# Attention and SwiGLU in one kernel: v's first loads issued by GpSimd, the planner's model of transfers in flight, and new ranks

## The chip, the cores and the metric

The kernel runs on one core of a Trainium2 chip. The metric is the device time of one execution in microseconds. Engines are named as in the profile: PE is TensorE (PEld its weight loads), DVE is VectorE, ACT is ScalarE, POOL is GpSimd, SP is SyncE, which only issues DMA transfers here. A name with a q behind it (SPq) is that engine's instruction queue.

## The reference

Attention over 8 batches of 8 heads, sequence 576, head size 64, with a mask that is causal in blocks of 64; its output, put side by side by heads, goes through a gated feed-forward layer on 4608 tokens of width 512, inner width 1536.

```python
scores = scale * np.matmul(q, k.transpose(0, 1, 3, 2))
mask = (pos[:, None] // 64) >= (pos[None, :] // 64)
scores = np.where(mask, scores, -1000000000.0)
attn = np.exp(scores - np.max(scores, axis=-1, keepdims=True))
attn = attn / (np.sum(attn, axis=-1, keepdims=True) + 1e-09)
o = np.matmul(attn, v)                         # [8, 8, 576, 64]
x = o.transpose(0, 2, 1, 3).reshape(4608, 512)
g = x @ w_gate                                 # [512, 1536]
out = (g * (1.0 / (1.0 + np.exp(-g))) * (x @ w_val)) @ w_out
```

q, k and v are 32-bit floats; the three weights are 64-bit and arrive as pairs of 32-bit words.

## The kernel before

**Work.** Attention goes by pairs of heads. The first two batches are cut into two stretches of the sequence, columns 0 to 256 and 256 to 576, so that the feed-forward layer can begin on the first 256 tokens; the other batches go whole. For the first stretch of batch 0 (four head pairs), each pair does this: q and k are loaded (line 401; q on SP's queue, k on ACT's), turned by TensorE (line 425) and copied out of PSUM by ACT (line 433); the scores are products on TensorE (line 451), masked by ACT (line 493); the maximum over the keys, which lie along the partitions, is taken by copies and maxima (lines 496, 716, 719) and then by POOL with one all-reduce over partitions for each of the two heads (line 723); DVE subtracts (line 747), ACT takes the exponential (line 751); TensorE multiplies with v and with ones, for the sums (line 829); DVE inverts and divides (lines 858 to 865); the result is split into a rounded part and a rest (lines 345 and 348).

**v.** `load_v` (lines 768 and 773) brings v of one head pair, two transfers of 64 KB for the stretch 0 to 256. There are two tiles for v at that time, each with room for two such pairs.

**Weights.** Each of 12 slices of the three weights is 512 KB, loaded at line 953 into one of five raw tiles, one after another; ACT and DVE put the two words of each number together (lines 968 to 982) and split it into a rounded part and a rest (lines 987 and 990). The split w_out is stored to memory (lines 1006 and 1009) and read again later (line 1176).

**Feed-forward.** 18 tiles of 256 tokens. Each takes three products for a weight block: rounded by rounded, rounded by rest, rest by rounded (lines 1109 to 1111 for the gate and the value, 1201 to 1203 for the output), with ACT and DVE between them (lines 1143 to 1159).

**Order.** Every step is a task with an engine, a cost in microseconds, a rank and the buffers that it needs. `in_order` plays the whole program through once, while the kernel is built: each engine in turn takes, of the tasks that are ready and have buffers, the one with the lowest rank, and the order so found is the order of each engine's instructions. The chip then runs each engine strictly in that order. Ranks are numbers written at the top: FIRST for the head pairs of the cut stretches, V_OF added to them for v, AHEAD and PIECES for the weights, SIDE for the first tiles' feed-forward, SHIFT, LATER, LEAD and EAGER for attention further back. PATIENCE bounds how long a run of feed-forward products may keep others waiting, `spare` how early a buffer may be counted on. Most buffers are handed out in the order in which they were first named (IN_TURN). A transfer costs its issuing engine 0.5 us an issue in the plan and lands after the share of the DMA engines that its size takes:

```python
if t.moves:
    queue = max(queue, end + 0.65) + t.moves
    done = queue + t.late
```

**Fillers.** Where the plan leaves TensorE a gap of over 0.3 us, `keep_busy` puts small matmuls of ones into it (line 1418), by the gap's length, that nothing reads.

Of the kernel before, what the change touches and what calls it, by code (L numbers as in the profile page):

```python
# [18 lines left out]
def kernel(  # L19
# [17 lines left out]
    nc = tc.nc  # L37
# [3 lines left out]
    P = 128  # L41
# [4 lines left out]
    SP = NKC * P  # L46
# [3 lines left out]
    XT = 256  # L50


    LEAD, EAGER = 6.5924, 0.1229

    SUMS = 2

# [3 lines left out]

    FINE = 4

    AHEAD = {(0, 0): -7.0107, (0, 1): 36.1085, (0, 2): -18.8912, (1, 0): 31.7427, (1, 1): -31.9799, (1, 2): 0.9815}
    SHIFT = {2: (7.4686, 5.1562, 10.9114, -4.5382), 3: (1.9556, -4.9491, 4.9621, -5.9019)}
    LATER = 10.5257
    V_OF = {0: (-22.086, 29.9358, 35.7938, -10.0705), 256: (-24.4193, 26.1695, 18.0768, -3.5685)}

    PIECES = [
        (-21.3689, -13.7546, 20.5567),
        (11.7941, 27.8219, -4.5726),  # L70
        (49.6885, 13.4156, 26.3321),
        (11.7183, 15.2197, -1.7579),
        (-18.0985, -44.9945, -47.4415),
        (31.6729, 24.8955, 16.7936),
        (60.2941, 42.2325, 2.1654),
        (-33.4359, -22.1211, 23.695),
        (-12.0038, 4.2143, -2.4693),
        (-8.6318, -21.6194, -14.638),
        (-12.3513, 22.147, -26.7278),
        (-43.9322, -25.5975, 15.0576),  # L80
    ]

    SIDE = (-30.9587, 40.07)

    PATIENCE = 63.9495
    FILL = 0.6

    FIRST = {
        0: [(0, 256, (-51.44, -5.5901, -6.4061, 10.6381)), (256, 576, (-51.1247, -24.9988, -31.7586, 0.8861))],
        1: [(0, 256, (6.1693, 18.1885, 17.2184, -3.8483)), (256, 576, (-0.9978, 12.9756, 15.3541, 29.1059))],  # L90
    }
    TILES = [XT] * (NT // XT)

# [220 lines left out]
    for i in range(7):  # L314
        n = 2**i
# [9 lines left out]
    if wide:  # L325
        for place in range(len(slots["ob"])):
            t = tiles_of("ob", place, "signs")[0].bitcast(F32).rearrange("p m t -> p (m t)")
# [28 lines left out]
    def attention(R, b, h, a, e, early, bufs, lane):  # L356
# [404 lines left out]

        ps = Buf("at", also=banks)

        def load_v():
            nf = e // P
            for j, hd in enumerate(heads):
                cols = slice(j * D, (j + 1) * D)
                nc.sync.dma_start(
                    out=vt[0][:, 2 * lane : 2 * lane + nf, cols],
                    in_=v[b, hd, 0 : nf * P].rearrange("(c p) d -> p c d", p=P),  # L770
                )
            if e > nf * P:
                nc.sync.dma_start(
                    out=vt[0][0 : e - nf * P, nf, :].rearrange("p (h d) -> p h d", h=2),
                    in_=v[b, h : h + 2, nf * P : e].rearrange("h p d -> p h d"),
                )

        vl = dma(R + ((V_OF[a][h // 2] if b == 0 else LATER) if early else 0.0), 512.0 * e, load_v, [], [vt], 3 if e % P else 2, packet=256)
        segs = [s for s in ((0, 2 * P), (2 * P, S)) if a <= s[0] and s[1] <= e]
        ends = []  # L780
        direct = b == 0
# [516 lines left out]
    def in_order():  # L1298


        import heapq

        engines = ("PE", "POOL", "DVE", "ACT", "SP")
        idle = {e: 0.0 for e in engines}
        could = {e: [] for e in engines}
        room = {tag: [(0.0, i) for i in range(len(s))] for tag, s in slots.items()}
        turn = dict.fromkeys(slots, 0)
        events = [0.6]
        for t in tasks:
            if not t.waits:  # L1310
                could[t.engine].append(t)
        order = []
        now = queue = 0.0
        mode, last, stage, two = "", None, "", False

        WARM = 7.0
        CHANGE = {
            "": {"columns": 0.1, "rows": 0.2},
            "up": {"down": 0.02, "split": 0.01, "columns": 0.13, "rows": 0.2},
            "down": {"up": 0.072, "split": 0.01, "columns": 0.13, "rows": 0.2},  # L1320
            "split": {"up": 0.072, "down": 0.05, "columns": 0.13, "rows": 0.2},
            "columns": {"up": 0.195, "down": 0.2, "split": 0.2, "rows": 0.19, "turn": 0.15},
            "rows": {"up": 0.195, "down": 0.2, "split": 0.2, "columns": 0.13, "rows": 0.04, "turn": 0.15},
            "turn": {"up": 0.04, "down": 0.04, "split": 0.04, "columns": 0.13, "rows": 0.2},
        }

        spare = {"PE": 0.5218, "DVE": 0.7384, "ACT": 0.6046, "POOL": 0.0, "SP": 0.0}

        def place(t, by):

            need, turns = [], dict(turn)
            for u in t.bufs:
                if u.place is not None:
                    continue
                if u.tag in IN_TURN and u.n != turns[u.tag]:
                    return False
                turns[u.tag] += 1
                for tag in (u.tag, *u.also):
                    free = [f for f in room[tag] if f[0] <= by and (tag, f) not in need]
                    if free:  # L1340
                        need.append((tag, min(free)))
                        break
                else:
                    return False
            new = [u for u in t.bufs if u.place is None]
            for u, (tag, f) in zip(new, need):
                turn[u.tag] += 1
                room[tag].remove(f)
                u.tag, u.place = tag, f[1]
            return True  # L1350

        while events:
            now = heapq.heappop(events)
            while events and events[0] <= now:
                heapq.heappop(events)
            for e in engines:
                if idle[e] > now:
                    continue
                cand = sorted(
                    (t for t in could[e] if t.ready <= now),  # L1360
                    key=lambda t: (not t.mode or t.mode != mode, t.rank, t.n)
                    if mode and e == "PE"
                    else (t.rank, t.n),
                )
                if e == "DVE" and idle["POOL"] > now:
                    cand = [t for t in cand if not t.port]
                if e == "POOL" and idle["DVE"] > now and two:
                    continue

                if e == "PE":  # L1370
                    spot = min(((f, tag, i) for tag in ("at", "gv", "po") for f, i in room[tag]), default=(now, "", 0))
                follow = [(now, t) for t in cand if t.prev is not None and t.prev is last]
                if any(t.ready < now - PATIENCE for t in cand):
                    follow = []
                for by, t in (*follow, *((by, t) for by in (now - spare[e], now) for t in cand)):
                    if t.ready <= by and place(t, by):
                        break
                else:
                    continue
                could[e].remove(t)  # L1380
                order.append(t)
                end = now + t.cost
                if e == "PE":
                    key = t.mode or t.stage
                    end, mode, last, stage = end + CHANGE[stage].get(key, 0.0), t.mode, t, key
                    t.gap, t.at, t.spot = now - max(idle[e], spot[0], 0.6), now, spot[1:]
                    if now < WARM:
                        end += end - now
                if e == "DVE":
                    two = t.port  # L1390
                idle[e] = end
                heapq.heappush(events, end)
                done = end + (0.2 if e == "PE" else 0.13)
                if t.moves:
                    queue = max(queue, end + 0.65) + t.moves
                    done = queue + t.late
                heapq.heappush(events, done)
                for u in t.bufs:
                    u.left -= 1
                    u.free_at = max(u.free_at, done)  # L1400
                    if not u.left:
                        room[u.tag].append((u.free_at, u.place))
                        heapq.heappush(events, u.free_at)
                for x in t.next:
                    x.waits -= 1
                    x.ready = max(x.ready, end if x.engine == e == "PE" else done)
                    if not x.waits:
                        could[x.engine].append(x)
        left = [t for e in engines for t in could[e]]
        assert len(order) == len(tasks), (len(order), len(tasks), [(t.engine, t.rank, t.fn.__qualname__) for t in left][:10])  # L1410
        return order
# [42 lines left out]
```

## Time and profile before

| what | value |
|---|---|
| median of 3 runs | 1167.11 us (1166.97 to 1167.42) |
| the profiled execution | 1170.11 us, its span 1168.3 us |
| TensorE busy | 1153.5 us, 99% of the span |
| VectorE, ScalarE, GpSimd busy | 743.6, 619.6, 321.1 us |
| moved by DMA | 197.44 MB, mean 169 GB/s |
| granted TensorE clock over the run | 0.997 |

Busy time of an engine is the time in which the profiler shows an instruction on it; matmuls overlap, so a busy TensorE need not be at its peak. The fillers count as busy. A row of the timeline gives start, duration, engine, line, operation, tiles, and in brackets how long the engine stood before it and what ended that. A DMA row on a queue shows the issue, not the landing. A row by stretches gives the stretch, its length, the busy time of each engine with the number of instructions, the granted TensorE clock as a share of full speed, the share of the 16 DMA engines and GB/s.

### The profile page before, as it was taken

How to read it: one execution, taken by the hardware profiler on the slowest of the kernel's cores; microseconds unless marked ns; L12 is line 12 of the kernel's file. 1: busy time of each engine (PE TensorE's matmuls, PEld its weight loads, DVE VectorE, ACT ScalarE, POOL GpSimd, SP SyncE). 2: the span in 40 equal slices, each digit the busy share in tenths (PEclk: the TensorE clock that was granted, in tenths of full speed). 3: DMA queues.
4: the chain of work that ended last, by engine and by line, in shares of the span. 5: the costliest groups of instructions: out<-in, count | busy, mean ns of one | idle time of the engine just before them, and what ended most of it. 6: DMA issues, size and time to landing. Idle time of an engine off the chain costs nothing.

```text
span 1168.3 us, 22310 instructions
## 1 busy us (share of the span) xinstructions
PE 1153.5 (99%) x8744; PEld 1038.0 (89%) x8744; DVE 743.6 (64%) x1230; ACT 619.6 (53%) x1114; POOL 321.1 (27%) x141
## 2 busy tenths in 40 slices
PE   7999999999999999999999999999999999999998
PEld 6778788889899989898998989898998989999997
DVE  4998898877697857576774747576575643323222
ACT  5889776745675655473745555473655422212111
POOL 3213100153525263334133423333133420000000
PEclk8999999999999999999999999999999999999999
DMA  7857756766557466653756565663664445444352
GB/s 185 228 153 213 192 189 226 213 197 170 159 150 210 116 183 181 195 151 114 189 166 197 140 182 144 199 159 123 175 196 149 144 142 170 145 162 138 142 172 100
DMA packets 266986, 197.44 MB, mean 169 GB/s; under 512 B 195264, under 2 KB 231376, under 8 KB 266880
## 3 DMA queue, kind: packets, MB, share of 16 engines
q1 hardware_dynamic: 264304, 195.29, 57.3%
q8 instruction: 69, 1.13, 0.4%
q10 hardware_dynamic: 2576, 0.72, 0.3%
q14 instruction: 37, 0.30, 0.1%
HBM read 171.57 MB, written 24.38 MB: 168 GB/s over the span
## 4 chain that ended last, share of the span: by engine, by line
PE 91%; ACT 4%; DMA 2%; DVE 2%; issue 1%; POOL 0%; SPq 0%; POOLq 0%; ACTq 0%
PE gv L1109 17%; PE gv L1111 16%; PE gv L1110 16%; PE at L829 8%; PE po L1201 8%; PE po L1203 7%; PE po L1202 7%; PE at L578 6%; PE at L451 1%; ACT sc L469 1%; PE at L1201 1%; DMA wo<-in_moe_w_gate_dram 1%; PE at L1202 1%; PE at L1203 1%; PE at L662 1%
## 5 line engine op out<-in xcount | busy, mean ns | idle before, releaser
L723 POOL PARTITION_ALL_REDUCE mx<-mx x80 | 140.6, 1805 | 395.3 <-DVE mx L719 184.6
L1109 PE MATMUL gv<-xhl,v_all 128*128 128x256 f32 x864 | 241.2, 279 | 0.1
L880 POOL PARTITION_ALL_REDUCE mx<-mx x48 | 178.3, 3768 | 228.2 <-DVE mx L719 214.6
L1111 PE MATMUL gv<-xhl,v_all 128*128 128x256 f32 x864 | 239.1, 277 | 0.0
L1110 PE MATMUL gv<-xhl,v_all 128*128 128x256 f32 x864 | 239.0, 277 | 0.0
L1146 DVE SCALAR_TENSOR_TENSOR t<-t,gv 128x512 f32<-128x512 f32 x108 | 73.9, 684 | 164.4 <-ACT t L1143 163.8
L1109 PEld LDWEIGHTS gv<-xhl,v_all 128*128 128x128 f32 x864 | 162.1, 188 | 3.5 <-issue 1.6
L1110 PEld LDWEIGHTS gv<-xhl,v_all 128*128 128x128 f32 x864 | 162.2, 188 | 0.5
L1111 PEld LDWEIGHTS gv<-xhl,v_all 128*128 128x128 f32 x864 | 162.2, 188 | 0.0
L1156 ACT CAST hhl<-t 128x512 fp32r<-128x512 f32 x108 | 67.1, 622 | 165.0 <-PE po L1202 93.5
L1201 PE MATMUL po<-wo,hhl 128*128 128x512 f32 x372 | 147.5, 397 | 0.0
L1203 PE MATMUL po<-wo,hhl 128*128 128x512 f32 x372 | 145.2, 390 | 0.3 <-DVE hhl L1159 0.3
L1202 PE MATMUL po<-wo,hhl 128*128 128x512 f32 x372 | 145.5, 391 | 0.0
L1159 DVE TENSOR_TENSOR hhl<-t,hhl 128x512 fp32r<-128x512 f32 x108 | 82.2, 763 | 90.3 <-ACT hhl L1156 90.0
L747 DVE TENSOR_TENSOR sc<-sc,mx 128x640 f32<-128x640 f32 (+6 forms) x168 | 122.8, 772 | 16.2 <-POOL mx L723 16.0
L1143 ACT ACTIVATE t<-gv 128x512 f32<-128x512 f32 x108 | 64.6, 598 | 119.3 <-PE gv L1111 114.3
L1151 DVE SCALAR_TENSOR_TENSOR t<-t,gv 128x512 f32<-128x512 f32 x108 | 73.9, 684 | 81.6 <-PE gv L1111 80.8
L1109 PE MATMUL gv<-xhl,g_even 128*128 128x256 f32 x432 | 123.8, 286 | 0.0
L751 ACT ACTIVATE sc<-sc 128x1024 f32<-128x1024 f32 (+3 forms) x104 | 105.7, 1032 | 31.8 <-DVE sc L747 31.2
L1111 PE MATMUL gv<-xhl,g_even 128*128 128x256 f32 x432 | 122.1, 283 | 0.0
L1110 PE MATMUL gv<-xhl,g_even 128*128 128x256 f32 x432 | 122.1, 283 | 0.0
L1109 PE MATMUL gv<-xhl,g_odd 128*128 128x256 f32 x432 | 120.5, 279 | 0.0
(173 smaller groups left out, 2465.9 us busy)
## 6 DMA issues: line engine op xcount, KB each, us to landing
wo<-wo_d SPq DMA_DIRECT2D x200, 512.0 KB
out_dram<-ob SPq DMA_DIRECT2D x35, 256.0 KB
v<-in_v_dram SPq DMA_DIRECT2D x64, 128.0 KB
xt<-x_d SPq DMA_DIRECT2D x64, 128.0 KB
rt<-r_d SPq DMA_DIRECT2D x128, 64.0 KB
qk<-in_q_dram SPq DMA_DIRECT2D x112, 72.0 KB
qk<-in_k_dram SPq DMA_DIRECT2D x104, 72.0 KB
x_d<-xu SPq DMA_DIRECT2D x24, 288.0 KB
```

What stands on the lines that cost most here:

```text
L723: nc.gpsimd.partition_all_reduce(m, m, channels=P, reduce_op=bass_isa.ReduceOp.max)
L747: nc.vector.tensor_tensor(piece(c), scores_of(c), m, ALU.subtract)
L751: nc.scalar.activation(x, x, AF.Exp)
L829: nc.tensor.matmul(ps[0][own(x), 1 - i if sums else i, q0 - s0 : s1 - s0], lhsT=ones if sums else vt[0][:, 2 * lane + c, own(x)], rhs=sc[0 ...
L880: nc.gpsimd.partition_all_reduce(m, m, channels=P, reduce_op=bass_isa.ReduceOp.add)
L1109: nc.tensor.matmul(o, lhsT=hi[:, d], rhs=xhi[:, 0:w], start=first, stop=False)
L1110: nc.tensor.matmul(o, lhsT=hi[:, d], rhs=xlo[:, 0:w], start=False, stop=False)
L1111: nc.tensor.matmul(o, lhsT=lo[:, d], rhs=xhi[:, 0:w], start=False, stop=last)
L1159: nc.vector.tensor_tensor(hh[1][:, 0:n], t[0][:, 0:n], hh[0][:, 0:n].bitcast(F32), ALU.subtract)
L1201: nc.tensor.matmul(po, lhsT=hi, rhs=whi, start=i + y == 0, stop=False)
L1202: nc.tensor.matmul(po, lhsT=hi, rhs=wlo, start=False, stop=False)
L1203: nc.tensor.matmul(po, lhsT=lo, rhs=whi, start=False, stop=i + y == NFC - 1)
```

## The change

Three things are done, all of them to what is issued where and in which order; no arithmetic is added or removed.

1. `load_v` takes its queue as an argument: for batch 0, stretch 0 to 256, GpSimd issues the eight transfers; all others stay on SP. The task is booked on POOL.
2. `in_order` keeps a list of eight times, `in_flight`. A transfer is played issue by issue: issue number n by SP or ACT starts no sooner than the landing of issue number n - 8. An issue by POOL costs twice the time and takes no part in the turns.
3. All ranks, LEAD, EAGER, LATER, PATIENCE, SIDE and `spare` have new values.

```diff
-    LEAD, EAGER = 6.5924, 0.1229
+    LEAD, EAGER = 5.2695, 1.0637
-    AHEAD = {(0, 0): -7.0107, (0, 1): 36.1085, (0, 2): -18.8912, (1, 0): 31.7427, (1, 1): -31.9799, (1, 2): 0.9815}
+    AHEAD = {(0, 0): -7.1143, (0, 1): 32.7291, (0, 2): -26.4529, (1, 0): 32.2582, (1, 1): -17.6111, (1, 2): -3.3862}
-    LATER = 10.5257
-    V_OF = {0: (-22.086, 29.9358, 35.7938, -10.0705), 256: (-24.4193, 26.1695, 18.0768, -3.5685)}
+    LATER = 3.3066
+    V_OF = {0: (-30.1506, 37.9633, 41.0176, -1.7015), 256: (-24.6985, 17.6488, 41.1206, -0.1297)}
...
-    PATIENCE = 63.9495
+    PATIENCE = 39.3039
...
-        0: [(0, 256, (-51.44, -5.5901, -6.4061, 10.6381)), (256, 576, (-51.1247, -24.9988, -31.7586, 0.8861))],
+        0: [(0, 256, (-55.7558, -1.8175, -4.7037, 13.4226)), (256, 576, (-49.0629, -29.9958, -41.3412, 1.2806))],
...
-        def load_v():
+        def load_v(queue=nc.gpsimd if b == a == 0 else nc.sync):
...
-                nc.sync.dma_start(
+                queue.dma_start(
...
-        vl = dma(R + (...), 512.0 * e, load_v, [], [vt], 3 if e % P else 2, packet=256)
+        vl = dma(R + (...), 512.0 * e, load_v, [], [vt], 3 if e % P else 2, "POOL" if b == a == 0 else "SP", 256)
...
+        in_flight, issued = [0.0] * 8, 0
...
-        spare = {"PE": 0.5218, "DVE": 0.7384, "ACT": 0.6046, "POOL": 0.0, "SP": 0.0}
+        spare = {"PE": 0.4096, "DVE": 0.7262, "ACT": 0.5782, "POOL": 0.0, "SP": 0.0}
...
                 end = now + t.cost
+                if t.moves:
+                    end, n = now, max(1, round(t.cost / 0.5))
+                    for _ in range(n):
+                        if e == "POOL":
+                            end += 2 * t.cost / n
+                            queue = max(queue, end + 0.65) + t.moves / n
+                            landed = queue + t.late
+                            continue
+                        end = max(end, in_flight[issued % 8]) + t.cost / n
+                        queue = max(queue, end + 0.65) + t.moves / n
+                        landed = in_flight[issued % 8] = queue + t.late
+                        issued += 1
...
                 if t.moves:
-                    queue = max(queue, end + 0.65) + t.moves
-                    done = queue + t.late
+                    done = landed
```

SHIFT, PIECES, SIDE and the rows of FIRST for batch 1 change in the same manner.

More of the change, by code (lines that the diff above doesn't have):

```diff
@@ L61 @@
     FINE = 4
-    AHEAD = {(0, 0): -7.0107, (0, 1): 36.1085, (0, 2): -18.8912, (1, 0): 31.7427, (1, 1): -31.9799, (1, 2): 0.9815}
-    SHIFT = {2: (7.4686, 5.1562, 10.9114, -4.5382), 3: (1.9556, -4.9491, 4.9621, -5.9019)}
-    LATER = 10.5257
-    V_OF = {0: (-22.086, 29.9358, 35.7938, -10.0705), 256: (-24.4193, 26.1695, 18.0768, -3.5685)}
+    AHEAD = {(0, 0): -7.1143, (0, 1): 32.7291, (0, 2): -26.4529, (1, 0): 32.2582, (1, 1): -17.6111, (1, 2): -3.3862}
+    SHIFT = {2: (1.75, -1.1716, 38.593, -6.5525), 3: (-4.8263, -5.9467, 11.997, -5.7384)}
+    LATER = 3.3066
+    V_OF = {0: (-30.1506, 37.9633, 41.0176, -1.7015), 256: (-24.6985, 17.6488, 41.1206, -0.1297)}
     PIECES = [
[L69 to L80, printed above, removed]
-    ]
-    SIDE = (-30.9587, 40.07)
-    PATIENCE = 63.9495
+        (-42.2477, -7.4078, 31.321),
+        (19.6584, 26.4752, -1.1002),
+        (45.1975, 13.7804, 42.9148),
+        (31.3974, 30.3821, -10.0232),
+        (-19.9421, -49.9897, -51.8768),
+        (32.5027, 18.8486, 12.5049),
+        (80.4454, 43.4201, 8.0835),
+        (-36.0942, -27.2001, 36.8872),
+        (-7.1654, 5.1657, -7.2183),
+        (-16.086, -25.0859, -4.9908),
+        (-16.2853, 35.6967, -8.3972),
+        (-54.782, -30.9951, 38.7919),
+    ]
+    SIDE = (-20.2791, 49.5735)
+    PATIENCE = 39.3039
     FILL = 0.6
     FIRST = {
-        0: [(0, 256, (-51.44, -5.5901, -6.4061, 10.6381)), (256, 576, (-51.1247, -24.9988, -31.7586, 0.8861))],
-        1: [(0, 256, (6.1693, 18.1885, 17.2184, -3.8483)), (256, 576, (-0.9978, 12.9756, 15.3541, 29.1059))],
+        0: [(0, 256, (-55.7558, -1.8175, -4.7037, 13.4226)), (256, 576, (-49.0629, -29.9958, -41.3412, 1.2806))],
+        1: [(0, 256, (3.4577, 25.759, 16.3827, -11.2353)), (256, 576, (-5.3054, 10.4811, 13.1627, 43.7195))],
     }
@@ L772, in load_v @@
             if e > nf * P:
-                nc.sync.dma_start(
+                queue.dma_start(
                     out=vt[0][0 : e - nf * P, nf, :].rearrange("p (h d) -> p h d", h=2),
@@ L776, in load_v @@
                 )
-        vl = dma(R + ((V_OF[a][h // 2] if b == 0 else LATER) if early else 0.0), 512.0 * e, load_v, [], [vt], 3 if e % P else 2, packet=256)
+        vl = dma(R + ((V_OF[a][h // 2] if b == 0 else LATER) if early else 0.0), 512.0 * e, load_v, [], [vt], 3 if e % P else 2, "POOL" if b == a == 0 else "SP", 256)
         segs = [s for s in ((0, 2 * P), (2 * P, S)) if a <= s[0] and s[1] <= e]
```

## The prediction

> **What bounds the kernel now.** I read the page's first part, then busy time by stretches, then the fillers, then the first 30 us engine by engine.
>
> ```profile
> span 1168.3 us, 22310 instructions
> PE 1153.5 (99%) x8744; PEld 1038.0 (89%) x8744; DVE 743.6 (64%) x1230; ACT 619.6 (53%) x1114; POOL 321.1 (27%) x141
> ...
> 200.00:400.00 200.00, 199.57 (x1520) 180.02 (x1519) 157.87 (x241) 126.64 (x224) 75.72 (x27) 1.00 0.67 186
> ...
> 0.00:120.00 120.00, 111.49 (x1013) 89.22 (x1013) 97.46 (x204) 97.01 (x189) 32.76 (x37) 0.97 0.73 195
> 120.00:200.00 80.00, 77.81 (x554) 64.70 (x553) 67.97 (x117) 57.99 (x98) 9.77 (x9) 1.00 0.64 193
> ```
>
> A stretch's row gives its length, then busy time of PE, PEld, DVE, ACT and POOL, granted TensorE clock, DMA share and GB/s. TensorE is the bound: of the 14.8 us of the span without a matmul (1168.3 - 1153.5), 8.5 lie in the first 120 us, 2.2 in the next 80, 0.4 in the 200 after, and 3.7 us are left for all the rest, so an order can win next to nothing behind 200 us. What can be won lies before it: those gaps, and the filler matmuls that the planner puts into gaps (line 1418):
>
> ```profile
> 0.00:8.00 8.00, 4.91 (x46) 4.63 (x46) 1.00 0.73 176
> 8.00:30.00 22.00, 6.38 (x67) 5.67 (x67) 0.84 0.74 192
> 30.00:45.00 15.00, 4.85 (x65) 4.16 (x66) 1.00 0.80 218
> 45.00:120.00 75.00, 4.64 (x58) 3.68 (x56) 1.00 0.71 193
> ```
>
> These are fillers alone: 15.9 us between 8 and 120 us, and in the first 30 us a lowered clock as well. The useful work of TensorE is the same before and after, so the end moves by what goes from gaps, fillers and slow clock. Where they come from shows in the DMA queue of SyncE (SP), in order of issue: start, time until the last of the row was out, what it loads.
>
> ```profile
> 0.73 0.96 SPq L768 DMA_DIRECT2D v<-in_v_dram  x2
> 1.74 0.97 SPq L401 DMA_DIRECT2D qk<-in_q_dram  x2
> 2.81 0.40 SPq L953 DMA_DIRECT2D wo<-in_moe_w_gate_dram  x1
> 3.55 5.74 SPq L401 DMA_DIRECT2D qk<-in_q_dram  x4
> 9.33 0.98 SPq L768 DMA_DIRECT2D v<-in_v_dram  x2
> 10.36 0.97 SPq L401 DMA_DIRECT2D qk<-in_q_dram  x2
> 11.38 2.00 SPq L768 DMA_DIRECT2D v<-in_v_dram  x4
> 13.42 1.61 SPq L953 DMA_DIRECT2D wo<-in_moe_w_val_dram  x1
> 15.15 0.95 SPq L401 DMA_DIRECT2D qk<-in_q_dram  x2
> ```
>
> Two free issues take 0.97 us, so 0.48 us each; four took 5.74 us, so SP stood there for 3.8 us, and again 1.1 us in w_val's single issue (1.61 against 0.40). The planner of before books 0.5 us an issue and no such stop, so it orders the engines as if these transfers landed earlier. What that costs, on ScalarE (ACT), VectorE (DVE) and TensorE:
>
> ```profile
> 18.20 0.78 ACT L968 ACTIVATE ob<-wo 128x512 f16<-128x512 f32 x1 [3.14 <-DMA wo<-in_moe_w_val_dram]
> 19.19 0.83 ACT L751 ACTIVATE sc<-sc 128x768 f32<-128x768 f32 x1
> ...
> 14.71 1.02 DVE L747 TENSOR_TENSOR sc<-at,mx 128x512 f32<-128x512 f32 x2 [2.00 <-POOL mx L723]
> ...
> 6.12 0.69 PE L425 MATMUL gv<-ident,qk 96*128 96x96 f32 x6 [0.67 <-DMA qk<-in_q_dram]
> 12.34 0.76 PE L425 MATMUL gv<-ident,qk 96*128 96x96 f32 x6
> 15.54 0.56 PE L1418 MATMUL gv<-ones 128*64 128x64 f32 x6
> 19.10 0.87 PE L425 MATMUL at<-ident,qk 96*128 96x96 f32 x4 [3.00 <-DMA qk<-in_q_dram]
> 19.91 1.86 PE L1418 MATMUL gv<-ones 128*64 128x64 f32 x15
> 21.46 0.69 PE L829 MATMUL at<-sc,v 128*64 128x256 f32 x1
> ```
>
> The first exponential (L751) had its input at 14.71 + 1.02 = 15.73, but stands behind L968 in ACT's order, which waits until 18.20 for w_val; it starts at 19.19, 3.46 us late. In the same stretch TensorE stands 3.00 us before the transposes of the second stretch's q, issued at 15.15 and used at 19.10. That gap has a tail:
>
> ```profile
> 18.00:19.00 1.00, 0.00 (x0) 0.00 (x0) 0.00 (x0) 0.80 (x2) 0.59 (x1) 0.82 1.18 265
> 24.00:25.00 1.00, 1.00 (x13) 1.00 (x9) 0.48 (x2) 0.97 (x2) 0.20 (x1) 0.50 0.89 230
> 26.00:30.00 4.00, 3.87 (x42) 2.85 (x41) 3.90 (x10) 3.77 (x7) 0.00 (x0) 1.00 0.80 194
> ```
>
> The granted clock falls at the end of the gap (0.82), is 0.50 still at 25 us, and 1.00 from 26 us on. From 26 us on DVE is busy 3.90 of 4.00 us: until there the transfers set the pace, from there the softmax and weight work does, and it starts earlier by as much as this chain starts earlier.
>
> **The change part by part.**
>
> *v's transfers.* Eight issues (four head pairs, two each) leave SP: three rows, and what SP gets back is the start of the next row less that of each: 1.01 + 1.03 + 2.04 = 4.08 us ahead of w_val's issue. No bytes go away. The same eight come on GpSimd (POOL), behind its start-up work and ahead of the first maximum:
>
> ```profile
> 3.63 0.98 POOL L329 MEMSET ob<- 128x512 f32 x2
> 12.03 2.65 POOL L723 PARTITION_ALL_REDUCE mx<-mx  x2 [7.41 <-DVE mx L719]
> ...
> L723 POOL PARTITION_ALL_REDUCE mx<-mx x80 | 140.6, 1805 | 395.3 <-DVE mx L719 184.6
> ...
> 8.00:10.00 2.00, 1.60 (x26) 1.34 (x22) 0.32 (x1) 1.12 (x3) 0.00 (x0) 1.00 0.49 105
> 10.00:12.00 2.00, 1.09 (x13) 0.98 (x14) 1.73 (x4) 1.50 (x4) 0.00 (x0) 1.00 0.59 133
> ```
>
> POOL is free from 4.61 to 12.03, 7.42 us. The trace has no DMA issue on POOL. Bounds: SP's 0.48 us (eight: 3.9, hidden) and POOL's mean custom instruction, 1.805 us (eight: 14.4, until 19.05). I take 1.0 us, which is also what the changed planner books (twice an SP issue), as the instruction is an issue and so nearer to the first: POOL is then free at 12.61, the first maximum 0.58 us late. I cost that at nothing: it puts the exponential's input at 16.3 and its end at 17.1, while TensorE is held until 17.05 by the next item. Without that cover it is 0.58 us. v itself is used at 21.46; even the last on POOL is out well before.
>
> [...]
>
> *w_val and the next q.* w_val's issue goes from 13.42 to about 9.3. It took 4.78 us to ACT's first use, so it lands near 14.1, and L968 no longer holds the exponential. The second stretch's q needs its buffer, which the transposes at 12.34 free at 13.10; SP is there by then, so the issue goes from 15.15 to 13.10, **2.05 us** earlier, and with the same 3.95 us to use TensorE goes on at 17.05. Bounds for this term: 0, if the planner puts something else into SP's place, and 3.46, if the exponential alone decides. I take 2.05, since TensorE takes its work in order and this wait ends last.
>
> *The clock.* TensorE's gap shrinks to about 1 us, so the clock stays up. What runs at 0.50 today, the first attention product (line 829):
>
> ```profile
> 20.00:24.40 4.40, 2.94 (x16) 2.40 (x16) 0.50 0.83 227
> 26.70:28.40 1.70, 1.52 (x16) 0.99 (x16) 1.00 0.72 168
> ...
> 29.95 1.03 PE L1418 MATMUL gv<-ones 128*64 128x64 f32 x14
> ```
>
> Sixteen take 2.94 us at half clock, 1.52 at full: **1.42 us**. The fifteen fillers before them took 1.86 us, and at the full clock's 1.03 for 14 they take 1.10: **0.76 us**. Both lie between the exponential and VectorE's inversion, on the chain.
>
> *The first q.* Its issue moves up 1.01 us; TensorE waited 0.67 for it at 6.12. Later transposes hang on the stops in SP's row at 3.55, which stay (w_gate's rank is still ahead of pairs 2 and 1). I take 0, bounds 0 and 1.01.
>
> *Turns at eight semaphores, in the planner.* No instruction of its own. Its effect is that a stop is booked where SP makes one, so the engines' orders fit the landings. It is what makes the second and third terms likely: a gap it foresees also gets fillers and keeps the clock. If it books stops too long, a filler costs 1.03/14 = 0.07 us, sixteen more 1.2 us.
>
> *Ranks, LEAD, EAGER, PATIENCE, spare.* Order only. After 200 us nothing can be won. Between 30 and 200 us they move every engine's order; bounds are the 2.2 us of gap in 120 to 200 with the 4.85 us of fillers in 30 to 45 as a gain, and one more gap like that at 16 (3.00 + 1.42 + 0.76 = 5.2 us) as a loss. I take 0.
>
> Sum: 2.05 + 1.42 + 0.76 = 4.23 us. The profiled execution took 1170.11 us, span 1168.3, so 1165.9 for one like it. It lies 3.0 us above the median of the runs, so against that median: 1167.11 - 4.23 = **1162.9 us**. The forecast's own range is 1159.5 (3.46 and 1.01 in place of 2.05 and 0, and 1 us of fillers) to 1164.7 (the 0.58 without its cover, and the 1.2 us of fillers). A measurement of this kernel can tell about 0.2%, 2.3 us, from no change.
>
> **The rivals.**
>
> *Hidden anyway: about 1167.* After 26 us DVE and ACT carry the pace (below), and what they get earlier may wait for weights or buffers; then gaps and fillers return between 30 and 60 us.
>
> ```profile
> 30.00:45.00 15.00, 14.20 (x153) 11.06 (x152) 14.53 (x31) 13.31 (x25) 5.26 (x4) 1.00 0.80 218
> ```
>
> For it: DMA share 0.80 in that stretch, and no byte is saved. Against it: DVE is at 14.53 of 15.00, so its work is what runs, and only its start is moved. It decides if 2 of the 4.23 us or more come back. Here also belongs that the new order makes nothing of SP's free time: 1167.1.
>
> *POOL becomes the bound: slower.* With c us for an issue on POOL, the first maximum starts at 4.61 + 8c instead of 12.03 and the exponential at 8.31 + 8c (15.73 today as far as its input goes) against 19.19. Even is c = 1.36; more than 2.3 us lost is c = 1.65. At POOL's 1.805 us an issue the exponential starts at 22.75, 3.56 us late: **1170.7 us**, with the slow clock unchanged. For it: POOL's main instruction costs that. Against it: an issue computes nothing.
>
> [...]
>
> *The new ranks open another gap.* 5.2 us against 4.23 won: 1168.1, no measurable change.
>
> **How the numbers follow.** Forecast 0.52; POOL's issues waiting for VectorE 0.07; hidden or no use made of it 0.16; POOL the bound 0.15; another gap 0.10. Faster takes the forecast, half of the case at 1164.9 and a quarter of the hidden one (some of it given back, not all): 0.60. Same: the other half, most of the hidden case and half of the gaps: 0.20. Slower: POOL and the worse gaps: 0.20. The range reaches down to 1158.0 (both upper bounds, 3.46 + 1.01 + 2.18 = 6.65, and 2.5 us of fillers) and up to 1169.5, past the gap case and into POOL's, leaving out about 2 in 10.
>
> **What would show it.** Right: SP's row has q first at 0.73 and w_val before 10.5; POOL has eight DMA issues from about 4.6 us and its first maximum before 13.5; the first exponential before 17.5; no stretch at clock 0.50 after 16 us; the first product of line 1109 near 27 instead of 30.9; fewer than 6.4 us of fillers in 8 to 30 us. Wrong: POOL's issues at 1.4 us or more each; a new TensorE wait of about 3 us with a clock of 0.50 behind it; fillers in 30 to 120 us above 9.5 us; or the first 30 us shorter and the end not, then it came back between 30 and 200 us.
>
> ```profile
> 30.91 0.39 PE L1109 MATMUL gv<-xhl,g_even 128*128 128x256 f32 x1
> ```

## The result and the profile after

| | before | after |
|---|---|---|
| median | 1167.26 us (1166.97 to 1169.63) | 1177.82 us (1174.37 to 1178.31) |
| ratio of the times, 95% interval | 1 | 1.0080 (1.0067 to 1.0094) |
| profiled execution, its span | 1170.11, 1168.3 us | 1178.06, 1176.3 us |

The kernel became slower, by 10.6 us in the medians. The forecast was 1162.9 us, with 1169.5 as the upper end of its range: the sign was wrong.

First the page's totals of the kernel after:

```profile
span 1176.3 us, 22354 instructions
PE 1158.5 (98%) x8766; PEld 1041.9 (89%) x8766; DVE 752.5 (64%) x1230; ACT 620.7 (53%) x1114; POOL 324.3 (28%) x149
```

Against before the span is 8.0 us longer: 3.0 us more without a matmul (1176.3 - 1158.5 = 17.8 against 14.8) and 5.0 us more of busy TensorE. (The spans lie closer together than the medians, since the profiled execution of before is 2.8 us above its median and that of after 0.2 us.) Its busy time by stretches after (length, then PE, PEld, DVE, ACT, POOL, clock, DMA share, GB/s):

```profile
10.00:20.00 10.00, 6.01 (x42) 4.92 (x40) 2.79 (x5) 4.24 (x9) 5.87 (x9) 0.54 0.72 202
20.00:30.00 10.00, 10.00 (x80) 8.36 (x76) 5.03 (x13) 6.81 (x13) 4.62 (x5) 0.61 0.48 121
0.00:120.00 120.00, 108.92 (x973) 87.37 (x975) 92.20 (x196) 91.99 (x179) 38.28 (x44) 0.93 0.70 185
120.00:200.00 80.00, 80.00 (x586) 67.14 (x583) 72.99 (x123) 61.63 (x107) 11.18 (x9) 1.00 0.69 207
200.00:400.00 200.00, 197.42 (x1503) 176.03 (x1503) 155.73 (x235) 125.45 (x220) 72.65 (x26) 1.00 0.65 179
```

The clock in the first 120 us is 0.93 (0.97 before) and 0.54 to 0.61 between 10 and 30 us. The gaps of TensorE in the first 120 us are 11.1 us (8.5 before), 120 to 200 us has none (2.2 before), and 200 to 400 us has 2.6 us (0.4 before). The 36 stores of the output after, first and last start:

```profile
L1232 SPq DMA_DIRECT2D out_dram<-ob x36: 337/338/543, 220.1 to 1173.3; - x36
```

In before they go from 217.4 to 1165.6. The first store is 2.7 us late and the last 7.7. So one part of the loss lies in the start, and another behind 200 us, where the prediction said that nothing could be won and did not ask what could be lost. I take the start first.

The loss at the start is seen first on GpSimd. The timeline of POOL after:

```profile
1.39 2.48 POOL L768 DMA_DIRECT2D v<-in_v_dram  x3
7.27 0.73 POOL L768 DMA_DIRECT2D v<-in_v_dram  x1 [3.41 <-issue]
9.20 2.16 POOL L768 DMA_DIRECT2D v<-in_v_dram  x3 [1.20 <-issue]
12.80 0.73 POOL L768 DMA_DIRECT2D v<-in_v_dram  x1 [1.45 <-issue]
13.54 0.32 POOL L328 COPY ob<-ident 128x1 f32<-128x1 f32 x2
13.79 0.99 POOL L329 MEMSET ob<- 128x512 f32 x2
17.46 2.57 POOL L723 PARTITION_ALL_REDUCE mx<-mx  x2 [2.68 <-DVE mx L719]
```

The eight issues stand ahead of the zeroing of the two `ob` tiles (lines 328 and 329), which was done at 4.61 us before and is done at 14.78 now. The first maximum over partitions starts at 17.46 instead of 12.03. What waits for the zeroing is ScalarE; its timeline after:

```profile
7.80 1.09 ACTq L401 DMA_DIRECT2D qk<-in_k_dram  x2
8.94 0.71 ACT L433 ACTIVATE parts<-gv 128x288 f32<-128x288 f32 x2 [2.89 <-DMA qk<-in_k_dram]
14.35 0.77 ACT L968 ACTIVATE ob<-wo 128x512 f16<-128x512 f32 x1 [4.71 <-POOL ob L329]
...
24.01 0.84 ACT L751 ACTIVATE sc<-sc 128x768 f32<-128x768 f32 x1
```

Line 968 writes into `ob`, stands 4.71 us for its zeroing, and behind it in ACT's order stand the mask and the copies of the first pair's scores and of the next pairs' q and k (lines 493, 496, 433). The first exponential starts at 24.01 (19.19 before). TensorE after:

```profile
9.70 0.92 PE L451 MATMUL at<-parts,parts 64*128 64x256 f32 x8 [2.29 <-ACT parts L433]
...
17.69 1.22 PE L425 MATMUL gv<-ident,qk 96*128 96x96 f32 x6 [3.99 <-ACT parts L433]
...
24.18 0.90 PE L425 MATMUL at<-ident,qk 96*128 96x96 f32 x4
...
34.98 0.39 PE L1109 MATMUL gv<-xhl,g_even 128*128 128x256 f32 x1
```

Two new waits, both for ScalarE's copy (line 433), the feed-forward begins at 34.98 instead of 30.91, and the second stretch's q, which I had expected 2.05 us earlier than 19.10, is turned at 24.18. Three rows of the stretches after show when the clock fell and how long that lasted:

```profile
10.00:11.00 1.00, 1.00 (x14) 0.84 (x11) 0.00 (x0) 0.00 (x0) 1.00 (x2) 0.89 0.99 232
11.00:12.00 1.00, 1.00 (x10) 0.88 (x9) 0.00 (x0) 0.00 (x0) 0.36 (x1) 0.50 0.71 159
...
27.00:28.00 1.00, 1.00 (x11) 0.91 (x11) 0.60 (x2) 0.64 (x2) 1.00 (x2) 0.58 1.07 323
```

It was full until 10 us, fell behind the first of the two waits and was 0.50 in each microsecond from 11 to 27, and rose in the next; the second wait came in the middle of that.

SyncE's queue after, in order of issue:

```profile
0.74 0.90 SPq L401 DMA_DIRECT2D qk<-in_q_dram  x2
1.70 0.46 SPq L953 DMA_DIRECT2D wo<-in_moe_w_gate_dram  x1
2.20 7.52 SPq L401 DMA_DIRECT2D qk<-in_q_dram  x6
9.76 0.47 SPq L953 DMA_DIRECT2D wo<-in_moe_w_val_dram  x1
12.63 0.84 SPq L401 DMA_DIRECT2D qk<-in_q_dram  x2
```

That part came as forecast: q first, w_val at 9.76 (13.42 before, forecast about 9.3), the next q at 12.63 (15.15 before, forecast 13.10). It was of no use, since TensorE got nothing to do with it.

The fillers after (matmuls of line 1430 alone):

```profile
8.00:30.00 22.00, 5.89 (x50) 5.12 (x50) 0.61 0.60 161
30.00:45.00 15.00, 3.98 (x50) 3.29 (x50) 1.00 0.71 191
45.00:120.00 75.00, 6.36 (x80) 5.26 (x80) 1.00 0.72 191
```

Between 8 and 120 us they take 16.2 us (15.9 before): what was lost there are gaps and clock, not fillers. Between 30 and 120 us alone it is 10.3 us, above the 9.5 us that the prediction named as a sign of being wrong.

### The profile page after: what moved, and what is told of

Same layout as the page of the kernel before. It is cut to its first block, busy times and chain, and to the rows that moved or that the text cites. A ratio compares the mean times of both kernels' runs of the same rounds, so it can differ in the third digit from the quotient of the medians.

```text
span 1176.3 us, 22354 instructions
## 1 busy us (share of the span) xinstructions
PE 1158.5 (98%) x8766; PEld 1041.9 (89%) x8766; DVE 752.5 (64%) x1230; ACT 620.7 (53%) x1114; POOL 324.3 (28%) x149
## 4 chain that ended last, share of the span: by engine, by line
PE 75%; DVE 0%; DMA 0%; issue 0%; ACT 0%
PE gv L1109 14%; PE gv L1111 14%; PE gv L1110 14%; PE po L1201 7%; PE po L1202 7%; PE po L1203 7%; PE at L578 5%; PE at L829 5%; PE at L1201 0%; PE at L1202 0%; PE at L1203 0%; DMA wo<-wo_d 0%; DVE mx L719 0%; DVE parts L251 0%; DVE sc L747 0%
## 5 line engine op out<-in xcount | busy, mean ns | idle before, releaser
L1146 DVE SCALAR_TENSOR_TENSOR t<-t,gv 128x512 f32<-128x512 f32 x108 | 73.9, 684 | 153.2 <-ACT t L1143 152.8
L1109 PE MATMUL gv<-xhl,g_odd 128*128 128x256 f32 x432 | 120.6, 279 | 0.0
L1111 PE MATMUL gv<-xhl,g_odd 128*128 128x256 f32 x432 | 119.4, 276 | 0.0
```

What stands on the lines that cost most here:

```text
L1109: nc.tensor.matmul(o, lhsT=hi[:, d], rhs=xhi[:, 0:w], start=first, stop=False)
L1111: nc.tensor.matmul(o, lhsT=lo[:, d], rhs=xhi[:, 0:w], start=False, stop=last)
L1146: nc.vector.scalar_tensor_tensor(t[0][:, 0:n], t[0][:, 0:n], 1.0, pg[0][:, 0:n], ALU.add, ALU.mult)
```

## The experiments

Theory A: what makes the kernel slow is GpSimd's order, with v's issues ahead of the zeroing of `ob` and of the first maximum. Theory B: the start is about even, and the new ranks lose the time later. Theory C, formed behind runs 2 to 4: each set of ranks fits one plan, and whatever changes the plan costs far more than the part under test. Ratios are to the kernel before, with a 95% interval.

**1. The zeroing off GpSimd.** The kernel after, with one instruction on VectorE, which has little to do at that time, in place of the copy and the zeroing of each `ob` tile.

```diff
-            nc.gpsimd.tensor_copy(t[:, 0:1], ident[:, 0:1])
-            nc.gpsimd.memset(t, 0.0)
+            nc.vector.memset(t, 0.0)
```

> The changed kernel, with the start-up zeroing of the two ob tiles (two copies, two memsets) taken from GpSimd and done by two memsets on VectorE; all else as changed. Theory A (GpSimd's order: the eight v issues stand ahead of that zeroing, ScalarE's first step on w_gate waits for the zeroed tile until 14.35 us, and the first maximum with it until 17.46): ScalarE's step at about 9.7, the first all-reduce at about 13.6, when the v issues are out, the first exponential near 20 instead of 24.0, 1171 to 1174 us. Theory B (the new ranks lose the time later on): the start shortens and the end does not, 1176 to 1178 us.

Measured: 1168.24 us, ratio 1.0004 (0.9993 to 1.0016). From 1.0080 that is 9.6 us less in the medians, 8.9 us by the ratios, by about 1 us of work moved to another engine, and more than theory A expected. Its profiled execution is the slowest of its ten, 1172.98 us, with a mean clock of 0.994 (0.999 or 1.000 in the nine others), and only its start is read here. GpSimd's first maximum, and ScalarE:

```profile
14.15 2.06 POOL L722 PARTITION_ALL_REDUCE mx<-mx  x2 [0.20 <-issue]
```

```profile
9.54 0.78 ACT L967 ACTIVATE ob<-wo 128x512 f16<-128x512 f32 x1
...
19.93 0.84 ACT L750 ACTIVATE sc<-sc 128x768 f32<-128x768 f32 x1
```

Line 967 (968 before) runs at 9.54 instead of 14.35, the first maximum at 14.15, the exponential at 19.93. Theory A is shown for this part of the loss. The v issues themselves lie about as in the kernel after (the last at 13.22, 12.80 there), and the first maximum still starts directly behind them.

**2 to 4. The queue changed with the plan.** Three kernels in which the planner books v on another engine than its ranks were made for: the kernel after with v on SP (2), the kernel before with v on POOL (3), and the latter with the zeroing on VectorE (4).

```diff
 2: -  def load_v(queue=nc.gpsimd if b == a == 0 else nc.sync):
    +  def load_v(queue=nc.sync):
    -  vl = dma(..., "POOL" if b == a == 0 else "SP", 256)
    +  vl = dma(..., "SP", 256)
 3: -  def load_v():
    +  def load_v(queue=nc.gpsimd if b == a == 0 else nc.sync):
    -  vl = dma(..., packet=256)
    +  vl = dma(..., "POOL" if b == a == 0 else "SP", 256)
 4: 3, and line 329 on VectorE as in 1
```

> The changed kernel with v's first eight transfers issued and booked on SyncE again; the new planner and the new ranks stay. Theory A: the zeroing is back at 4.6 us and the first all-reduce near 12, 1164 to 1169 us, about as before the change or better. Theory B: the ranks still cost, 1172 to 1178 us.

> The kernel before, with v's first eight transfers issued and booked on GpSimd and nothing else changed (old ranks, old planner). Theory A: the same order on GpSimd as in the changed kernel, the first all-reduce near 17, 1173 to 1178 us. Theory B: 1165 to 1169 us.

> The same as the one with the old ranks and v on GpSimd, and the zeroing of the ob tiles on VectorE. Theory A: first all-reduce near 13.6, some 3 to 5 us faster than with the zeroing on GpSimd, 1168 to 1172 us. Theory B: as with the zeroing on GpSimd within 1.5 us.

Measured: 1185.30 us, ratio 1.0155 (1.0139 to 1.0170); 1186.48, 1.0168 (1.0151 to 1.0185); 1182.87, 1.0136 (1.0119 to 1.0152). All three are 15 to 19 us slower than before, kernel 2 too, in which GpSimd has no issue at all; none of the three lies in a range that either theory gave. One row of stretches of kernel 3, and two of kernel 2, show part of where:

```profile
60.00:90.00 30.00, 26.74 (x202) 19.03 (x200) 22.71 (x44) 23.09 (x46) 4.11 (x4) 0.89 0.54 155
```

```profile
60.00:90.00 30.00, 28.48 (x249) 22.12 (x248) 28.97 (x54) 26.13 (x54) 5.53 (x4) 1.00 0.75 198
200.00:400.00 200.00, 197.75 (x1525) 176.82 (x1524) 142.63 (x222) 111.14 (x197) 69.42 (x24) 1.00 0.61 176
```

Gaps far behind the start, at a place that the edit doesn't touch, since every engine's order was made anew. In kernel 2 the feed-forward even begins earlier than before (29.27 against 30.91), but its stores go from 220.0 to 1181.0, 961.0 us against 948.2 before. These runs say nothing of v's queue. For the rest I kept the planned order of each kernel and changed only what is emitted.

**5, 6 and 12. The order of before, kept.** The planner books v on SP as before; only the queue is GpSimd's (5); the same with the zeroing on VectorE (6); and the zeroing alone, with v on SP (12).

```diff
 5: -  def load_v():
    +  def load_v(queue=nc.gpsimd if b == a == 0 else nc.sync):
    -                nc.sync.dma_start(
    +                queue.dma_start(
 6: 5, and line 329 on VectorE as in 1
12: line 329 on VectorE as in 1, nothing else
```

> The kernel before with its own order kept: the plan still books v's first eight transfers on SyncE, only the issuing queue is GpSimd's. Theory A (GpSimd's order): ScalarE's first weight step held until about 14, first all-reduce near 17 instead of 12.0, 1172 to 1177 us. Theory C (what the replanned kernels lost, 15 to 19 us, is that ranks fit one plan only): with the order kept it is well under the 1186 us of the replanned one. Were it the issue by GpSimd itself that costs, it would be near 1186.

> The same order of before, v issued by GpSimd, and the zeroing of the ob tiles on VectorE. Theory A: first all-reduce near 13.9, bound by the last v issue; 4 to 7 us less than with the zeroing on GpSimd, 1166 to 1170 us. If the zeroing is not what holds: no change of more than 1 us.

> Control: the kernel before with only the zeroing of the ob tiles moved to VectorE; v on SyncE. There it ended at 4.6, four microseconds ahead of w_gate's landing at 8.8, so theory A expects no change: 1166.5 to 1168.5 us. Were VectorE's zeroing a gain by itself: 1163 to 1165.

Measured: (5) 1171.08 us, ratio 1.0023 (1.0013 to 1.0034), less than theory A expected; (6) 1166.17, 0.9982 (0.9973 to 0.9991); (12) 1167.87, 1.0000 (0.9991 to 1.0009). Kernel 5 and kernel 3 send v through the same queue and differ in the plan alone: 15 us. Kernels 9 (below) and 2 do the same with the other ranks: 13 us. That shows theory C for these two sets of ranks. Kernel 5 against 6 is the zeroing alone, 4.9 us; in 5 it held ScalarE as in the kernel after:

```profile
12.95 0.79 ACT L968 ACTIVATE ob<-wo 128x512 f16<-128x512 f32 x1 [3.94 <-POOL ob L329]
```

Kernel 12 shows that the zeroing costs nothing on GpSimd as long as nothing stands ahead of it. So 6 against 12 is v's queue by itself, a gain of about 2 us (0.9982 against 1.0000).

Does what is won at the start last? The rows of the 36 stores of the output, first and last start, of before, 5 and 6:

```profile
L1232 SPq DMA_DIRECT2D out_dram<-ob x36: 337/338/881, 217.4 to 1165.6; - x36
```

```profile
L1232 SPq DMA_DIRECT2D out_dram<-ob x36: 337/340/545, 218.0 to 1166.3; - x36
```

```profile
L1231 SPq DMA_DIRECT2D out_dram<-ob x36: 337/340/536, 213.5 to 1161.7; - x36
```

From the first store to the last it is 948.2, 948.3 and 948.2 us: with one order, what is won or lost by the first store stays until the end.

**9. The order of after, kept, v on SP.**

```diff
-        def load_v(queue=nc.gpsimd if b == a == 0 else nc.sync):
+        def load_v(queue=nc.sync):
```

> The changed kernel with its own order kept (the plan still books v's first eight transfers on GpSimd) but SyncE issuing them. Theory A: GpSimd's issues are the loss, so zeroing at 4.6 us again, first all-reduce at 12 to 13.5, 1166 to 1171 us, near the kernel before. Theory B (the new order itself is slow): 1175 us or more.

Measured: 1171.85 us, ratio 1.0037 (1.0025 to 1.0050), a little above what theory A gave. The issue on GpSimd with all that it brings costs 6 us in this order (5.0 by the ratios). At the start there is another wait: SP's four issues of v stand ahead of q, and TensorE waits for that.

```profile
5.45 4.87 SPq L768 DMA_DIRECT2D v<-in_v_dram  x4
```

```profile
13.19 0.74 PE L425 MATMUL gv<-ident,qk 96*128 96x96 f32 x6 [3.46 <-DMA qk<-in_q_dram]
```

But the 4 us above before are not lost there: the feed-forward begins at 30.62 (30.91 before) and the first store is at 214.6 (217.4), while the last is at 1167.2 (1165.6). They lie behind the first store, and that is theory B. From the first store to the last, the order of after takes 952.0 to 953.2 us in its seven traces (after, 1, 7, 8, 9, 11, 14), the order of before 948.1 to 948.3 us in six (before, 5, 6, 10, 12, 13). What makes the difference was followed no further than the gaps between 200 and 400 us: 1.4 to 2.6 us against 0.3 to 0.5.

**7, 8, 10 and 11. The other waits, one after the other.** In kernel 1 the first maximum still waits for the last v issue, and ScalarE for the last two k issues (8.94 against 6.60). Kernel 8 is 1 with v of the third and fourth pair in the plan issued behind the first maximum; 7 also issues the fourth pair's k on SP. Kernels 10 (order of before) and 11 (order of after) have the zeroing on VectorE, that k on SP, and those two pairs' v behind the third maximum.

```diff
 7, 10, 11: -  load_qk(1, nc.scalar)
            +  load_qk(1, nc.scalar if h < 6 else nc.sync)
            ...
 7, 8:      +  on_pool = [t for t in order if t.engine == "POOL"]
            ...
            +  order = [t for t in order if t not in on_pool[2:4]]
            +  at = order.index(on_pool[5]) + 1
            +  order[at:at] = on_pool[2:4]
 10, 11:    +  vs = [t for t in order if t.fn.__name__ == "load_v"][2:4]
            +  most = [t for t in order if t.engine == "POOL" and t not in vs and t.fn.__name__ != "load_v"]
            +  order = [t for t in order if t not in vs]
            +  at = order.index(most[5]) + 1
            +  order[at:at] = vs
```

> The changed kernel's plan with three waits taken away: zeroing of ob on VectorE; the fourth head pair's two k issues on SyncE instead of ScalarE, where they wait for w_gate's landing and hold the first copy out of PSUM until 8.94; v of the last two pairs issued behind the first maximum. Theory A with these two further waits: first scores near 7.4, first all-reduce near 11, TensorE's clock not below 0.9 for more than 3 us, 1161 to 1166 us. If the two further waits are covered by w_gate's own landing: 1166.5 to 1169, as with the zeroing alone.

> The changed kernel with the zeroing on VectorE and v of the last two pairs issued behind the first maximum. The first all-reduce, held until 14.15 by GpSimd's last issue, then starts near 12.6; if GpSimd's issues are a bound by themselves, 1165.5 to 1167.5 us; if not, 1168 as with the zeroing alone.

> The order of before, v issued by GpSimd, zeroing on VectorE (1166.2 us), and two more waits taken away: the fourth pair's two k issues on SyncE instead of ScalarE, and v of the last two pairs issued behind the third maximum, not between the first two. Expected from the waits: first scores near 7.4 instead of 9.2, first all-reduce near 11 instead of 13.4, maxima not held by GpSimd's issues, 1162.5 to 1165.5 us. If another transfer then ends last: 1165.5 to 1167.5.

> The same three waits taken away in the changed kernel's order. Theory A: the second maximum no longer at 20.5 as with v behind the first maximum, 1163.5 to 1167 us. If the changed order is slower by itself beyond the start: 1167 to 1169.

Measured: (7) 1169.79 us, ratio 1.0016 (1.0005 to 1.0027); (8) 1172.14, 1.0031 (1.0020 to 1.0042); (10) 1169.45, 1.0013 (1.0003 to 1.0023); (11) 1171.91, 1.0035 (1.0022 to 1.0048). All four missed. The first maximum did come at 10.6 to 12.1 us, but a later wait took its place. In 7, and in 8 likewise, the four moved issues held the second maximum, and TensorE with it; POOL and PE of kernel 7:

```profile
19.70 0.73 POOL L767 DMA_DIRECT2D v<-in_v_dram  x1 [3.79 <-issue]
20.47 4.16 POOL L722 PARTITION_ALL_REDUCE mx<-mx  x4
```

```profile
23.64 1.22 PE L424 MATMUL at<-ident,qk 96*128 96x96 f32 x6 [4.08 <-DVE sc L746]
```

In 10, and in 11 likewise, v itself came too late, as the two pairs moved were the last in the planned order of loads and not the last to be used; TensorE in 10:

```profile
23.26 1.08 PE L828 MATMUL at<-sc,v 128*64 128x256 f32 x2 [3.12 <-DMA v<-in_v_dram]
```

**13 and 14. All three at once.** Zeroing on VectorE, the fourth pair's k on SP, v of the two head pairs used first ahead on GpSimd (four issues), v of the other two behind the third maximum; 13 in the order of before, 14 in that of after.

```diff
 +  vs = sorted((t for t in order if t.fn.__name__ == "load_v"), key=lambda t: t.n)[:4]
 +  most = [t for t in order if t.engine == "POOL" and t not in vs]
 +  order = [t for t in order if t not in vs]
 +  at = order.index(most[5]) + 1
 +  order[at:at] = vs[2:]
 +  order[0:0] = vs[:2]
```

> The order of before, zeroing on VectorE, the fourth pair's k issues on SyncE; on GpSimd v of pairs 0 and 1 at the start, which the first two products with v use, and v of pairs 2 and 3 behind the third maximum. If the new wait for v (3.1 us, with a slow clock behind it) was all that took back what the three waits gave: first product of the gate near 26.5, 1162 to 1165 us. If the start no longer sets the end by then: 1166 to 1168.

> The same in the changed kernel's order. If GpSimd's issues, the zeroing behind them and ScalarE's wait for its own k issues were the whole loss: 1163 to 1166.5 us. If the changed order loses a few microseconds by itself, as it did with v on SyncE (1171.9): 1167 to 1171.

Measured: (13) 1165.04 us, ratio 0.9977 (0.9965 to 0.9988), a little faster than both kernels, and not clearly faster than 6 (0.9982); (14) 1167.67, 0.9996 (0.9987 to 1.0005). Stretches and TensorE's first feed-forward product of 13:

```profile
10.00:20.00 10.00, 8.74 (x95) 7.12 (x96) 6.26 (x14) 7.22 (x16) 5.88 (x6) 1.00 0.90 226
20.00:30.00 10.00, 8.87 (x99) 6.82 (x97) 9.79 (x23) 9.50 (x18) 5.42 (x7) 1.00 1.02 285
```

```profile
26.21 0.39 PE L1108 MATMUL gv<-xhl,g_even 128*128 128x256 f32 x1
```

This execution has no slow clock (over the seven the mean clock goes from 0.995 to 1.000), and the feed-forward begins at 26.21, 4.7 us earlier than before; the first store comes 6.7 us earlier. Kernel 14 starts nearly as early (its row has 26.51) but doesn't end so; a stretch of 14, its stores, and then the stores of 13:

```profile
200.00:400.00 200.00, 198.56 (x1518) 178.75 (x1517) 156.13 (x237) 124.08 (x217) 76.72 (x28) 1.00 0.62 174
```

```profile
L1231 SPq DMA_DIRECT2D out_dram<-ob x36: 337/338/543, 211.9 to 1164.0; - x36
```

```profile
L1231 SPq DMA_DIRECT2D out_dram<-ob x36: 337/338/536, 210.7 to 1159.0; - x36
```

0.3 us between them at the first product, 1.2 at the first store, 5.0 at the last, in these two executions (2.6 in the medians): that again is theory B's part, the order of after by itself.

**What the runs add up to.** By the ratios, along one path: v on GpSimd with the zeroing off it, 0.9982, which is -2.1 us; then the order of after, 1.0004, +2.6 us; then the zeroing back on GpSimd, 1.0080, +8.9 us. The same zeroing costs 4.9 us in the order of before, so about 4 us of it come from the new order together with it. In kernel 5 the exponential starts 4.32 us behind the first maximum (16.13 to 20.45), in the kernel after 6.55 (17.46 to 24.01), where ScalarE has two more steps ahead of it (lines 972 and 433) and TensorE's products run at half clock (0.50); no run separates the two. By another path, the order of after alone is +4.3 us (9, 1.0037), and v on GpSimd with the zeroing behind it +5.0 us. So of the 9.3 us by the ratios the new order has 2.6 to 4.3, and v's issues on GpSimd, with what stands behind them, 5.0 to 6.7.

## Why the prediction was wrong

- **The step that failed** is in "v's transfers": "The same eight come on GpSimd (POOL), behind its start-up work". They came ahead of it. Lines 328 and 329 stand ahead of all tasks in the program's text, and I took that for the engine's order. The copy of line 328 has to have `ident`, which VectorE makes by 3.32 us in the trace of before and by 3.61 in that of after; v's issues don't need it and were placed at 1.39. (That they were placed first for this reason is inferred.) From there it goes on to ScalarE's line 968, the first maximum and the exponential. The fall of the clock at 10.8 us follows another wait, for k (below): the profiled execution of experiment 1 has it too (0.54 between 10 and 20 us). Experiment 1 gives this step 9.6 us in the medians, 8.9 us by the ratios.
- **The size of an issue.** "I take 1.0 us": an issue is 0.73 us, less than taken. But GpSimd stands between them, 3.41, 1.20 and 1.45 us, so eight last from 1.39 to 13.53, 1.52 us each. Even without the zeroing the first maximum would have started at 14.15 (experiment 1), not at 12.61.
- **"I cost that at nothing"**, with TensorE's wait until 17.05 as cover: the cover was there only if ScalarE was on time. The exponential ended at 24.85 instead of 17.1.
- **The rival "POOL becomes the bound"** was the right mechanism at the right place, with too low a chance and too low a price. By its own sum, 1.52 us each would put the first maximum at 16.77 and give 1168.4; it started at 17.46, and the rival knew neither the zeroing behind the issues nor the mask and copies behind ScalarE's wait nor the clock.
- **The two terms of the gain** were right as far as SyncE goes (w_val at 9.76, the next q at 12.63) and did not arrive, as TensorE's wait moved to ScalarE. What they were worth with the zeroing out of the way, and the wait for k (below) still there, is shown by experiment 6: -1.9 us in the medians against the forecast -4.2. (Experiment 13 has -3.2 us, but with k moved and v split as well.)
- **The clock's 1.42 and 0.76 us** were read from one execution, in which the clock was at 0.50 for 6.8 us. The median that the sum starts from also holds executions without that: of those of before measured beside the experiments, 51 had a mean clock of 0.997 or less and average 1168.2 us, 18 had 0.999 or more and average 1167.7. By that I estimate the two terms at 0.6 us in a median, not 2.18. Kernel 12, with the order of before, stood for 2.10 us at the same wait for q in its profiled execution and kept a clock of 1.00.
- **A wait that I had not seen.** With v off SP's queue, w_gate is issued at 1.70 us (2.81 before), and the issues of the last two k, on ACT, stand until 7.80 and 8.57 (4.55 and 6.24 before). They hold line 433 to 8.94 and TensorE for 2.29 us. With that k on SP (experiment 13) line 432 runs at 6.44. In both traces each of the two starts 0.02 us behind the landing of an earlier k of ACT's: issued at 1.73 and 2.25 and landed at 7.78 and 8.55 after, issued at 1.78 and 2.29 and landed at 4.53 and 6.22 before. It is not w_gate's landing that they wait for, as I had put it ahead of experiment 7; that one, at 8.37, is what SP's next q waits for (4.5 us). What made those two k land later was not shown by a run of its own.
- **"Ranks ... I take 0"** was 2 to 4 us too low (in the medians 2.1 by 1 against 6, 2.6 by 14 against 13, 4.0 by 9 against 12), and "after 200 us nothing can be won" overlooked that there something can be lost: 2.6 us of gaps instead of 0.4.
- **"Hidden anyway"** is refuted for what reaches the first store: the 36 stores keep their distance to the end in before, 5, 6 and 13. **"POOL's issues waiting for VectorE"** (0.07, the case at 1164.9) is shown by no run: two rows that follow each other on VectorE after show it idle over nearly the whole time of the issues:

```profile
3.33 0.28 DVE L321 TENSOR_SCALAR ident<-t 128x128 f32<-128x128 f32 x1
15.16 0.69 DVE L977 SCALAR_TENSOR_TENSOR wo<-wo,ob 128x512 int32<-128x512 int32 x1 [11.55 <-ACT ob L968]
```

GpSimd's stops of 3.41, 1.20 and 1.45 us lie between 3.87 and 12.80, VectorE is idle from 3.61 to 15.16. So VectorE ended none of these stops; each ended 0.31 us behind the landing of an earlier v transfer (last section).

Left open: what makes GpSimd stop, and whether fewer bytes or larger pieces would take the stops away; and where the new order loses its time behind the first store.

One reading in the prediction is off and no term rests on it: w_val's issue stood for 1.2 us by the two figures given (1.61 against 0.40), not 1.1.

## What to carry to other kernels

Before moving work to an engine that looks idle, find out in which order that engine will run it, from a trace and not from the program's text: here an instruction that waited for something fell behind eight that didn't, and what it fed (a 1 us zeroing for ScalarE) fell with it. Move such start-up work away first, and split what is added, so that the engine's own urgent work comes between. With ranks fitted to one plan, test a part with the order kept; a new plan alone moved the time by 13 to 15 us here. And look at more than one execution before pricing a slow clock: here it came in some executions of a kernel and not in others.

## What the runs showed of the hardware

**GpSimd's issues stop in threes.** Wherever GpSimd has all eight in a row (after, 1, 3, 4, 5, 6), three issues go one behind the other, the fourth comes 5 to 6 us after the first; three more follow (in 4 with 0.18 us between the last two), and the eighth comes 2.8 to 4.4 us after the fifth: 3, 1, 3, 1. Two rows of the kernel after, duration of an issue (min, median, max, in ns) and time to landing:

```profile
L768 POOL DMA_DIRECT2D v<-in_v_dram x8: 720/726/1019, 1.4 to 12.8; - x8
...
DMA to landing us min/median/max: 2.9/4.7/6.5
```

In the kernel after the first five of these transfers (64 KB in rows of 256 bytes) land at 6.96, 8.89, 9.51, 10.18 and 12.49 us. The three issues behind a stop, the fourth, the fifth and the eighth, start at 7.27, 9.20 and 12.80: each 0.31 us behind the landing of the third issue before it. The sixth and the seventh, without a stop, start at 9.92 and 10.64, 0.41 and 0.46 us behind such a landing. On SP the same issue has a median of 0.47 us in the kernel before.

**The clock was low for multiples of 3.4 us.** If the clock is taken as full up to one point and 0.50 from there, the row at 10 us in the result above (0.89) puts the fall at 10.78 us, and the row at 27 (0.58) the return at 27.84, 17.06 us later. In before, the rows at 18 (0.82) and at 25 (0.76) give 18.64 and 25.48, 6.84 us. In experiments 6 and 10 the rows of 10 us (0.96 and 0.87 up to 20 us; 0.83 from 20 to 30) give 3.4 us each. These are 5, 2, 1 and 1 times 3.41 us. Ahead of the fall at 10.78 TensorE stood for 2.29 us, until 9.70, and was then busy for 1.08; in experiment 12 it stood for 2.10 us until 18.68 and the clock stayed at 1.00. What brought the clock down in the one and not in the other was not shown.
